# Fused block attention, gated MoE and routed experts on one core: the fourth group's scores from f16 halves, the weight preparation written later, and new anchors for work on ScalarE and VectorE

## The chip, the cores and the metric

The kernel runs on one core of a Trainium2 chip. The metric is the device time of one execution in microseconds (us); lower is better. TensorE (PE) multiplies matrices, VectorE (DVE) and ScalarE (ACT) do elementwise work and reductions, GpSimd (POOL) and SyncE (SP) mostly issue transfers (DMA). Engines run side by side and wait for each other by semaphores.

## What is computed

```python
def reference(**kwargs):                      # q, k, v: (8, 8, 576, 64)
    attn_out = _attn_ref(**attn_kwargs)       # softmax(q k^T / 8 + block mask) v, blocks of 64
    B, H, S, D = attn_out.shape
    x = np.ascontiguousarray(attn_out.transpose(0, 2, 1, 3)).reshape(B * S, H * D)   # 4608 x 512
    x = _moe_ref(x=x, **moe_kwargs)           # ((x @ w1) * (x @ w2)) @ w3 @ w_out
    return _moe2_ref(x=x, **moe2_kwargs)      # logits = x @ w_gate; each token goes to one of 8
                                              # experts by capacity; relu(x @ w1[e]) @ w2[e]
```

Inputs and outputs are f32.

## The kernel before

The first half of the program (to about 722 us) holds the attention and the products with w1 and w2. Attention is cut into 32 head pairs `n` (four for each of the eight batches `b`), and each pair into two parts, which gives 64 half steps `h`. A half step makes scores on TensorE (`tiles`, tile S in PSUM, two buffers), takes the row maxima on VectorE (`maxima`, tile nb), exponentials with row sums on ScalarE (`exp`, tile E), and splits the normalised result into an f16 high half (`high`, mostly ScalarE) and an f16 low half (`low_`, VectorE), both in tile P. A DMA transposes P (`transP`, tile PT), and about a half step later TensorE multiplies PT by v (`pv`, tile PV). That product is split in turn into halves of tile xT: ScalarE writes the high half, then VectorE the low half (`lo`). When all four pairs of a batch are there, `moe_unit` multiplies xT by one 128-column block of w1 and of w2 (24 matmuls, three f16 products per block of the contraction), ScalarE copies one result (`copy_`, tile a_sb) and VectorE multiplies it with the other (`gate_`, tile g). There are 128 such units, two in most half steps. They and the small products of `total` share three PSUM buffers named ab.

q and k come in groups of two pairs (`GROUPS`, `load_qk`, tile qk32, two buffers). Groups below `GF` use the f32 data as they are, in one f32 product. From group `GF` on, `qk_scale` squares q and k on ScalarE (`sq`, tile junk), lets TensorE add up the sums over partitions (`total`, a product with a tile of ones, reading tile qm), makes a power-of-two scale on VectorE (`fin`, tile qp), and splits q and k into f16 halves: `high_half` on ScalarE and `low_half` on VectorE (tile qkT). The scores are then three f16 products. The same squares, totals and splits serve v (`scale_v`, `prep_v`), w_out (`wo_chunk` decodes and squares it, `wo_half` splits it, `wo_turn` turns it by DMA) and w3 (`w3_chunk`); `w34` multiplies the two and writes W3 x w_out to memory for later.

The order of the work is written by hand in units of half steps. `at(p, f)` puts f at place p, `defer(d, f)` at d after the present place, and the program is emitted in order of these places. From half step `HS` = 14 on, TensorE's own order is exactly this one. The other engines' orders come from a scheduler that may move an instruction ahead of others. `behind(key, f)` binds it: what f issues stays behind the newest instruction that is kept under that key ("a" the copy of a unit, "g" its gate, "m" the maxima, "e" the exponentials). `spread` puts ScalarE and VectorE pieces at one of the two places of each half step that `PLACES` lists, each bound behind its key.

The last half of the program (routing of the tokens and the experts) is not touched.

## Time and profile before

| | us |
|---|---|
| median of three runs | 1444.08 (1442.85 to 1445.35) |
| the profiled execution | 1445.89 |
| its span in the trace | 1444.2 |

The span is the time from the first to the last recorded instruction. The profiled execution is a run of its own, 1.8 us above the median. A busy engine is one with an instruction in flight. A row of a wait names the engine that was idle and the instruction of another engine that ended the idle time. The granted clock is 1.00 where TensorE runs at 2.4 GHz throughout and 0.50 where it runs at 1.2 GHz.

### The profile page before, as it was taken

To read this page: it belongs to the slowest core of one execution; us is meant where nothing else is said; L and a number is where in the kernel's file an instruction comes from. 1 tells how busy PE (TensorE), PEld (TensorE's weight loads), DVE (VectorE), ACT (ScalarE), POOL (GpSimd) and SP (SyncE) were. 2 spreads that over 40 slices of the span, in tenths; PEclk is the share of its full clock that TensorE was granted. 3 is DMA by queue.
4 is the path that set the end of the run, shared out by engine and by line. 5 is a ranking of instruction groups with operands and counts; after the bars stand their busy time and mean duration, and the time that the engine had idled before them with its cause. 6 is when DMAs were issued, how large, how long until landed. Compare 5 with 4: busy or idle time off the path is not lost. (4 is left out here: it accounts for less than half of the span.)

```text
span 1444.2 us, 31956 instructions
## 1 busy us (share of the span) xinstructions
PE 1316.7 (91%) x12461; PEld 909.5 (63%) x12461; DVE 963.7 (67%) x2866; ACT 950.7 (66%) x2223; POOL 114.5 (8%) x136
## 2 busy tenths in 40 slices
PE   4689779899999999999999899999889999999997
PEld 3356457676767666766776566666576566666663
DVE  7998788788878888777514577777454456354530
ACT  7887787878878788776634465455346667675641
POOL 0000000000000000010001111111032211110001
PEclk6789999999999999999999999999989999999999
DMA  9888779887978876698999978979585686565200
GB/s 287 199 180 198 182 161 203 180 186 170 175 180 166 190 199 137 149 224 212 227 287 227 234 171 211 203 206 202 154 155 142 158 199 144 177 161 153 74 30 37
DMA packets 383814, 257.45 MB, mean 178 GB/s; under 512 B 260784, under 2 KB 344752, under 8 KB 382640
## 3 DMA queue, kind: packets, MB, share of 16 engines
q1 hardware_dynamic: 370464, 213.44, 62.1%
q0 software_dynamic: 11520, 39.87, 12.3%
q8 instruction: 97, 1.59, 0.5%
q10 hardware_dynamic: 1680, 2.11, 0.4%
q14 instruction: 53, 0.43, 0.1%
HBM read 130.84 MB, written 39.86 MB: 118 GB/s over the span
## 5 line engine op out<-in xcount | busy, mean ns | idle before, releaser
L453 PE MATMUL ab<-xT,w1h 128*128 128x288 f16 x1536 | 218.8, 292 | 20.4 <-DVE xT L429 14.0
L453 PE MATMUL ab<-xT,w2h 128*128 128x288 f16 x1536 | 214.5, 290 | 3.6 <-ACT w34o L718 2.0
L1333 PE MATMUL pe<-xT,ewa 128*128 128x288 f16 (+2 forms) x1728 | 193.0, 275 | 1.6 <-ACT xT L1301 0.9
L453 PEld LDWEIGHTS <-w1h 128*128 128x128 f16 x1536 | 148.3, 101 | 67.8 <-issue 26.6
L1351 PE MATMUL pe<-ewb,h 128*128 128x512 f16 (+1 forms) x960 | 189.3, 379 | 0.0
L453 PEld LDWEIGHTS <-w2h 128*128 128x128 f16 x1536 | 152.4, 99 | 46.2 <-issue 5.2
L1333 PEld LDWEIGHTS <-ewa 128*128 128x128 f16 x1728 | 157.7, 99 | 36.1 <-issue 2.0
L369 DVE SCALAR_TENSOR_TENSOR P<-E,rr,P 128x128 f16<-128x128 f32 (+4 forms) x288 | 155.7, 575 | 15.5 <-ACT P L365 15.4
L1351 PEld LDWEIGHTS <-h 128*128 128x128 f16 (+1 forms) x960 | 85.4, 101 | 98.8 <-issue 2.6
L349 ACT ACTIVATE E<-S,nb,cc 128x384 f32<-128x384 f32 (+4 forms) x216 | 136.3, 639 | 2.1
L365 ACT ACTIVATE P<-E,rr 128x384 f16<-128x384 f32 (+2 forms) x224 | 121.2, 603 | 8.2 <-DVE rr L354 2.1
L1141 PE MATMUL px<-W34h,gh 128*128 128x512 f32 x288 | 120.0, 417 | 3.3 <-ACT gh L1162 3.3
L1141 PE MATMUL px<-W34h,gl 128*128 128x512 f32 x288 | 119.8, 416 | 3.5 <-DMA gl<-g 3.5
L1141 PE MATMUL px<-W34l,gh 128*128 128x512 f32 x288 | 119.5, 415 | 0.0
L341 DVE TENSOR_REDUCE nb<-S 128x2 f32<-128x768 f32 (+3 forms) x128 | 101.1, 814 | 3.8 <-PE S L327 3.4
L423 PE MATMUL PV<-PT,v 128*64 128x128 f16 (+1 forms) x2880 | 88.2, 218 | 16.8 <-DMA PT<-P 15.7
L423 PEld LDWEIGHTS <-v 128*64 128x64 f16 x2880 | 77.3, 114 | 35.2 <-issue 27.2
L1336 DVE SCALAR_TENSOR_TENSOR h<-pe,h 128x288 f16<-128x288 f32 (+2 forms) x144 | 57.7, 419 | 46.9 <-ACT h L1335 46.0
L1354 ACT ACTIVATE y<-pe,s 128x512 f32<-128x512 f32 x36 | 24.7, 687 | 95.0 <-PE pe L1351 65.8
L1291 DVE SCALAR_TENSOR_TENSOR x<-xg,xsc,x 128x512 f16<-128x512 f32 x36 | 27.1, 751 | 84.0 <-ACT x L1290 84.0
L1335 ACT ACTIVATE h<-pe 128x288 f16<-128x288 f32 (+2 forms) x144 | 52.6, 377 | 44.5 <-PE pe L1333 41.6
L1159 ACT ACTIVATE gl<-g 128x1024 fp32r<-128x1024 f32 x36 | 37.9, 1056 | 64.7 <-DMA g<-gd 64.7
(298 smaller groups left out, 2255.6 us busy)
## 6 DMA issues: line engine op xcount, KB each, us to landing
g<-gd SPq DMA_DIRECT2D x36, 512.0 KB, 5.5
gl<-g POOLq DMA_DIRECT2D x36, 512.0 KB, 5.6
raw<-in_moe_w_dram SPq DMA_DIRECT2D x32, 512.0 KB, 4.7
esa<-in_moe_w_dram SPq DMA_DIRECT2D x8, 2048.0 KB, 9.9
esb<-in_moe_w_dram SPq DMA_DIRECT2D x8, 2048.0 KB, 11.3
gd<-g SPq DMA_DIRECT2D x56, 288.0 KB, 3.5
g<-gd SPq DMA_DIRECT2D x14, 1152.0 KB, 7.8
v<-in_v_dram SPq DMA_DIRECT2D x8, 1280.0 KB, 6.7
```

Source lines behind the costliest of these rows:

```text
L341: newest["m"] = nc.vector.tensor_reduce(nb[:, 0, x:x + 2], ps[:, :, o:o + N], axis=AX.X, op=ALU.max)
L349: newest["e"] = nc.scalar.activation(d["e"][:, cols[x]], pf_[:, cols[x]], AF.Exp, bias=nb[:, 1, x:x + 1], scale=c[:, 0:1], accum_out=sums[ ...
L365: nc.scalar.activation(hi, d["e"][:, cols[x]], AF.Copy, scale=r[:, 1, x:x + 1])
L369: nc.vector.scalar_tensor_tensor(lo, d["e"][:, cols[x]], r[:, 1, x:x + 1], hi, op0=ALU.mult, op1=ALU.subtract)
L423: nc.tensor.matmul(ps[hh * 64:hh * 64 + 64, c0:c0 + w], vt[:, zv, hh, j, :], s, start=z == 0 and j == 0, stop=z == 2 and j == nj - 1)
L453: nc.tensor.matmul(p[:, :288], w[:, zw, cc, :], x[:, zx, cc, c0:c0 + 288], start=first, stop=cc == 3 and zw == 1)
L1141: nc.tensor.matmul(p, gh[a][:, f], W34[b][:, f], start=f == 0 and a + b == 0, stop=f == 7 and a == 1)
L1159: nc.scalar.activation(gh[1], g, AF.Copy, scale=-1.0)
L1333: nc.tensor.matmul(p[:, :n], w1[:, a, cc, f * P:(f + 1) * P], t[:, 4 * b + cc, x], start=cc == 0 and a + b == 0, stop=cc == 3 and a == 1)
L1335: nc.scalar.activation(h[:, 0, f, x], p[:, :n], AF.Relu)
L1336: nc.vector.scalar_tensor_tensor(h[:, 1, f, x], p[:, :n], 0.0, h[:, 0, f, x], op0=ALU.max, op1=ALU.subtract)
L1351: nc.tensor.matmul(p[r0:r1], h[:, a, f, k_ * P + r0:k_ * P + r1], EW[e, "b"][0][:, b, f], start=f == 0 and a + b == 0, stop=f == 7 and a == 1)
```

## The change

`GF` goes from 4 to 3, so the fourth group (pairs 6 and 7, half steps 10, 11, 14 and 15) is split into halves and scored by three f16 products; `qk_scale` for it is written at place 8.2. The scale of group 4 moves from 13.95 to 14.42, that of group 5 from 16.4 to 14.95, and those of the later groups by a tenth. Group 4's squares, and the pieces that ScalarE gets by `spread`, are now bound behind the exponentials ("e", place .42) or behind xT's high half ("x", place .07) instead of behind the copies of a unit. The first maxima of a half step are bound behind xT's low half ("xl"). The decode, split and turn of w_out, the decode of w3 and `w34` are written six to seven half steps later, with w3 at 3.2 half steps a chunk instead of 4.

```diff
--- before.py
+++ after.py
@@ -26,7 +26,7 @@
 TS = 13
 HS = 14
 UL = 112
-GF = 4
+GF = 3
 DVE_HI = (2,), (2,)
 TH = 5
 TB = 15
@@ -158,7 +158,7 @@
         with tc.issue_after(newest[key].ins):
             f(*a)
 
-    PLACES = {"a": ((.42, "a"), (.76, "a")), "g": ((.3, "m"), (.58, "g")), "g5": ((.58, "g"), (.92, "g"))}
+    PLACES = {"a": ((.07, "x"), (.42, "e")), "g": ((.3, "m"), (.58, "g")), "g5": ((.58, "g"), (.92, "g"))}
 
     def spread(key, p, f, *a, soon=False):
         p = max(p, now[0])
@@ -187,7 +187,7 @@
             else:
                 spread(key, now[0] + .1, low_half, soon=key != "g")
 
-        spread("a", p, high_half)
+        spread("a", p, high_half, soon=key != "g")
 
     gate = {}
     qk32, qkT, vhl, xT, PT = {}, {}, {}, {}, {}
@@ -277,7 +277,7 @@
                                                op0=ALU.mult, op1=ALU.mult)
             for z in range(2):
                 split(T[:, z, 0, :w], T[:, z, 1, :w], qk32[g][:, z, :w], s[:, z:z + 1], .14,
-                      then=lambda: end(d2), key="g5" if g == 5 else "g")
+                      then=lambda: end(d2), key="g5" if g == 4 else "g")
             pq[g] = s, c, T
 
         done = []
@@ -293,9 +293,9 @@
             if g + 2 < len(GROUPS):
                 load_qk(g + 2)
 
-        if g == 5:
-            defer(.02, behind, "a", sq, 0)
-            defer(d0, behind, "a", sq, 1)
+        if g == 4:
+            defer(0, behind, "e", sq, 0)
+            defer(.02, behind, "e", sq, 1)
             return
         spread("a", now[0], sq, 0)
         spread("a", now[0] + d0, sq, 1)
@@ -369,7 +369,10 @@
                 nc.vector.scalar_tensor_tensor(lo, d["e"][:, cols[x]], r[:, 1, x:x + 1], hi, op0=ALU.mult,
                                                op1=ALU.subtract)
 
-            defer(nb_at, maxima)
+            if now[0] > HS + 1 and nb_at < .15:
+                defer(nb_at, behind, "xl", maxima)
+            else:
+                defer(nb_at, maxima)
             for x in range(k_):
                 defer(ex_at + .05 * x, exp, x)
                 defer(hi_at + .02 * x, high, x)
@@ -426,11 +429,14 @@
         x = xT[b]
 
         def lo():
-            nc.vector.scalar_tensor_tensor(x[:, 1, hp, i0 * 64:i1 * 64], ps[:, :w], 2.0 ** -TS,
-                                           x[:, 0, hp, i0 * 64:i1 * 64], op0=ALU.mult, op1=ALU.subtract)
+            newest["xl"] = nc.vector.scalar_tensor_tensor(x[:, 1, hp, i0 * 64:i1 * 64], ps[:, :w], 2.0 ** -TS,
+                                                          x[:, 0, hp, i0 * 64:i1 * 64], op0=ALU.mult, op1=ALU.subtract)
             held.remove("v")
 
-        defer(.12, lambda: nc.scalar.activation(x[:, 0, hp, i0 * 64:i1 * 64], ps[:, :w], AF.Copy, scale=2.0 ** -TS))
+        def hi():
+            newest["x"] = nc.scalar.activation(x[:, 0, hp, i0 * 64:i1 * 64], ps[:, :w], AF.Copy, scale=2.0 ** -TS)
+
+        defer(.12, hi)
         defer(.13, lo)
 
     lg, lgT, gg = {}, {}, {}
@@ -700,7 +706,7 @@
             m = sm.tile([P, 1], F32, name="w3m")
             wo["T", f] = wo["p3"].tile([P, 2, 1024], F16, name="w3h", bufs=2)
             spread("a", now[0], ssq, w3, m, wo["T", f][:, 1])
-            defer(.8, total, m, .06, use)
+            defer(.7, total, m, .06, use)
 
         decode(("3", f, h), w3[:, h * 512:h * 512 + 512], squares if h else lambda: None)
 
@@ -802,24 +808,25 @@
         at(8 * b + 4.5, scale_x, b)
         at(8 * b - 1.4 if b else .34, scale_v, b)
         if b + 1 < B:
-            at(8 * b + (4.1 if b < 2 else 5.35), load_v, b + 1)
-    for p, g in ((6.1, 2), (8.1, 3), (13.1, 4), (16.1, 5)):
+            at(8 * b + (4.1 if b < 2 else 5.62), load_v, b + 1)
+    for p, g in ((5.1, 2), (7.1, 3), (13.05, 4)):
         at(p, load_qk, g)
-    at(13.95, qk_scale, 4, .1, .5, 0)
-    at(16.4, qk_scale, 5, .36, .3, 0)
+    at(8.2, qk_scale, 3, .15, .3, 0)
+    at(14.42, qk_scale, 4, 0, .56, 0)
+    at(14.95, qk_scale, 5, .3, .6, 0)
     for g in range(6, len(GROUPS)):
         b = g // 2 - 1
-        at(8 * b + (6.9 if g % 2 else 4.9), qk_scale, g, .3, .6 if g % 2 else .45, 1.02)
+        at(8 * b + (7 if g % 2 else 5), qk_scale, g, .3, .62, 0)
     for f in range(8):
         at(2 + .7 * f, prep_w, f)
-        at(9.2 + .75 * f, wo_chunk, f)
-        at(16.2 + .25 * f, wo_half, f)
-        at(18.4 + .5 * f, wo_turn, f)
-        at(23.5 + 4 * f, w3_chunk, f, 0)
-        at(24.9 + 4 * f, w3_chunk, f, 1)
-        at(27.58 + 4 * f, w34, f)
-    at(15.8, wo_split)
-    at(22.95, wo_gate)
+        at(16.2 + .75 * f, wo_chunk, f)
+        at(22.6 + .25 * f, wo_half, f)
+        at(26.2 + .5 * f, wo_turn, f)
+        at(29.6 + 3.2 * f, w3_chunk, f, 0)
+        at(30.6 + 3.2 * f, w3_chunk, f, 1)
+        at(int(33.28 + 3.2 * f) + .42, w34, f)
+    at(22.2, wo_split)
+    at(30.8, wo_gate)
     at(55.97, late_open)
     for h in range(UL // 8):
         at(56.6 + .9 * h, alone, "l", late_run, h)
```

TensorE, around the sum of group 4's squares (`ab<-qm,ones`): w1h_73 is the first weight tile of the second unit in half step 14, w1h_74 that of the first unit in half step 15. Before:

```order
L423 LDWEIGHTS v_1061
L423 MATMUL PV<-PT_2100,v_1061 64x64
L145 MATMUL ab<-qm,ones 128x2
L453 LDWEIGHTS w1h_73
L453 MATMUL ab<-xT,w1h_73 128x288
```

and after the change:

```order
L387 LDWEIGHTS q_108
L387 MATMUL S<-qkT,q_108 128x64
L145 MATMUL ab<-qm,ones 128x2
L459 LDWEIGHTS w1h_74
L459 MATMUL ab<-xT,w1h_74 128x288
```

The sum stood ahead of the second unit of half step 14; now it stands behind that unit and behind the scores of half step 15.

ScalarE in half step 14, from its exponentials on (`E` 128x576). Tile qk_2128 is group 4's, wo is w_out, dec a decoded weight. Before:

```order
L349 ACTIVATE E,sums<-S,nb,c_110 128x576
L197 ACTIVATE wo_1480,wom<-wo_1478 128x512
L365 ACTIVATE P_120<-E,rr 128x576
L563 ACTIVATE dec<-raw 128x512
L365 ACTIVATE P_120<-E,rr 128x512 x2
L197 ACTIVATE junk,qm<-qk_2128 128x1152
L365 ACTIVATE P_119<-E,rr 128x576
L433 ACTIVATE xT<-PV 128x192
L197 ACTIVATE junk,qm<-qk_2128 128x1152
L463 ACTIVATE a_sb<-ab 128x288
L197 ACTIVATE v_2305,vm<-v_121 128x1024
L184 ACTIVATE qkT<-qk_2128,qp 128x1152 x2
```

After the change, where group 4's tile is qk_2107:

```order
L349 ACTIVATE E,sums<-S,nb,cc 128x576
L197 ACTIVATE junk,qm<-qk_2107 128x1152
L469 ACTIVATE a_sb<-ab 128x288
L197 ACTIVATE wo_2528,wom<-wo_2526 128x512
L365 ACTIVATE P_120<-E,rr 128x512 x2
L569 ACTIVATE dec<-raw 128x512
L365 ACTIVATE P_119<-E,rr 128x576
L197 ACTIVATE junk,qm<-qk_2107 128x1152
L469 ACTIVATE a_sb<-ab 128x288
L437 ACTIVATE xT<-PV 128x192
L197 ACTIVATE v_2274,vm<-v_121 128x1024
L347 ACTIVATE nb<-nb,cc 128x2
```

The first square stands directly behind the exponentials and the second behind as many instructions as before. Nine instructions further down the order goes on, with the last of the exponentials of half step 15, the third square of v, group 5's first square (`qk_1458`) and only then group 4's two upper halves (`qkT<-qk_2107`):

```order
L349 ACTIVATE E,sums<-S,nb,cc 128x576
L197 ACTIVATE v_2274,vm<-v_121 128x1024
L197 ACTIVATE junk,qm<-qk_1458 128x1152
L184 ACTIVATE qkT<-qk_2107,qp 128x1152 x2
L469 ACTIVATE a_sb<-ab 128x288
```

Between the second square and these two halves there is now the work of a whole half step; before, there were two instructions.

VectorE at the start of half step 38, where batch 4's first unit waits for xT (the same at 30, 46 and 54). `nb<-S` are maxima, `xT<-PV,xT` is the low half. Before:

```order
L696 TENSOR_TENSOR w3f<-w3p,wgee 128x1
L341 TENSOR_REDUCE nb<-S 128x2
L369 SCALAR_TENSOR_TENSOR P_120<-E,rr,P_120 128x576
L343 TENSOR_REDUCE nb<-S 128x1
L429 SCALAR_TENSOR_TENSOR xT<-PV,xT 128x384
L77 TENSOR_SCALAR qp<-ab 128x2
```

and after the change:

```order
L702 TENSOR_TENSOR w3f<-w3p,wgee 128x1
L432 SCALAR_TENSOR_TENSOR xT<-PV,xT 128x384
L341 TENSOR_REDUCE nb<-S 128x2
L77 TENSOR_SCALAR qp<-ab 128x2
L343 TENSOR_REDUCE nb<-S 128x1
L179 SCALAR_TENSOR_TENSOR w3h<-w3d,w3p,w3h 128x1024
```

xT's low half has moved ahead of both maxima.

## Rows read from the trace of the kernel before

**Rows 1.** The page's first line.

```profile
span 1444.2 us, 31956 instructions
```

**Rows 2.** Stretches: length, busy us of each engine (x its instructions), granted clock, DMA.

```profile
core 0: us, PE busy (x) PEld busy (x) DVE busy (x) ACT busy (x) POOL busy (x), PEclk, DMA share, GB/s
0.00:158.97 158.97, 114.74 (x1112) 78.24 (x1113) 142.20 (x356) 128.37 (x331) 1.60 (x11) 0.83 0.87 214
158.97:228.22 69.25, 52.59 (x619) 38.19 (x620) 52.77 (x130) 53.91 (x129) 0.00 (x0) 0.90 0.78 173
228.22:291.60 63.38, 57.37 (x734) 43.88 (x731) 48.88 (x134) 50.86 (x121) 0.00 (x0) 0.95 0.95 193
291.60:365.62 74.02, 70.94 (x834) 51.02 (x832) 63.55 (x160) 61.17 (x148) 0.00 (x0) 1.00 0.80 180
365.62:623.88 258.26, 244.61 (x2964) 177.17 (x2959) 213.25 (x541) 213.10 (x519) 1.77 (x10) 1.00 0.76 167
623.88:721.85 97.97, 92.43 (x1144) 65.68 (x1138) 67.21 (x169) 62.84 (x167) 4.35 (x3) 0.97 0.98 231
...
170.80:176.40 5.60, 5.49 (x28) 3.65 (x28) 0.63 (x5) 2.02 (x5) 0.00 (x0) 0.60 0.48 89
...
201.90:206.80 4.90, 4.86 (x27) 3.28 (x28) 3.67 (x18) 4.83 (x17) 0.00 (x0) 0.65 0.55 139
...
216.20:220.80 4.60, 4.60 (x28) 3.04 (x25) 3.22 (x7) 1.98 (x7) 0.00 (x0) 0.63 1.07 268
```

**Rows 3.** Waits of PE, 158.9 to 721.9 us: total us, times, longest.

```profile
PE ab L453 <- DVE xT L429: 14.0, 9, 4.7
PE ab L145 <- ACT junk L197: 9.6, 2, 5.0
```

**Rows 4.** Waits of ACT, the same stretch and columns.

```profile
ACT nb L347 <- DVE nb L341: 71.0, 49, 6.3
```

**Rows 5.** Timeline of PE, half steps 14 to 18: start us, us, what, [idle before].

```profile
170.91 0.59 PE L145 MATMUL ab<-qm,ones 128*128 128x2 f32 x2 [5.02 <-ACT junk L197]
...
178.53 1.63 PE L453 MATMUL ab<-xT,w1h 128*128 128x288 f16 x12
...
201.94 0.38 PE L145 MATMUL ab<-qm,ones 128*128 128x2 f32 x2 [4.60 <-ACT junk L197]
...
215.53 0.50 PE L323 MATMUL S<-qkT 64*128 64x384 f16 x4 [2.79 <-DVE qkT L179]
```

**Rows 6.** Timeline of ACT, half steps 14 to 17.

```profile
163.72 0.83 ACT L349 ACTIVATE E<-S,nb,c 128x576 f32<-128x576 f32 x1
...
169.60 1.16 ACT L197 ACTIVATE junk<-qk 128x1152 f16<-128x1152 f32 x1
...
175.78 2.39 ACT L184 ACTIVATE qkT<-qk,qp 128x1152 f16<-128x1152 f32 x2
...
191.62 0.72 ACT L184 ACTIVATE wo<-wo,wop 128x512 f16<-128x512 f32 x1
...
196.77 1.16 ACT L197 ACTIVATE junk<-qk 128x1152 f16<-128x1152 f32 x1 [1.03 <-DMA qk<-in_q_dram]
```

**Rows 7.** Groups by shape on PE, 80 to 240 us: count, busy us, mean ns.

```profile
L323 PE MATMUL S<-qk 64*128 64x384 f32 x16 | 4.0, 576 | 0.9 <-ACT E L349 0.9
L323 PE MATMUL S<-qkT 64*128 64x384 f16 x24 | 2.8, 323 | 3.6 <-DVE qkT L179 2.8 <-ACT qkT L184 0.8
```

**Rows 8.** Timeline of PE: w34 in half step 35, units in 38 and 58.

```profile
397.95 5.34 PE L713 MATMUL ab<-wo,w3h 128*128 128x512 f16 x24
...
430.92 0.41 PE L453 MATMUL ab<-xT,w1h 128*128 128x288 f16 x2 [1.64 <-DVE xT L429]
...
651.61 0.64 PE L453 MATMUL ab<-xT,w1h 128*128 128x288 f16 x2 [4.67 <-DVE xT L429]
```

**Rows 9.** Timeline of ACT at the start of half step 38.

```profile
428.16 0.48 ACT L433 ACTIVATE xT<-PV 128x384 f16<-128x384 f32 x1
```

**Rows 10.** Timeline of DVE, the same place.

```profile
427.80 1.22 DVE L341 TENSOR_REDUCE nb<-S 128x2 f32<-128x1024 f32 x1
...
430.32 0.55 DVE L429 SCALAR_TENSOR_TENSOR xT<-PV,xT 128x384 f16<-128x384 f32 x1
```

## The prediction

> **What bounds the kernel now.** I read the table of stretches first [rows 2]. Until 159 us VectorE is busy for 142.2 us of 159.0, and TensorE for 114.7; the order of TensorE is not yet the written one there. From 158.97 (the scores of half step 14) to 721.85 us TensorE is the bound: it is idle for 69.25 − 52.59 = 16.7, 63.38 − 57.37 = 6.0, 3.1, 13.7 and 5.5 us in the five stretches A to E, 45.0 us together, while VectorE and ScalarE are busy for three quarters to seven eighths of each. The granted clock adds a loss: (1 − 0.90) × 69.25 = 6.9 us in A, 3.2 in B (0.95), 2.9 in E (0.97), none in C and D. This is an upper bound, since some of it falls on idle time. So 45.0 + 13.0 = 58 us is all that better order can give back there, and what comes after 721.85 us (722.4 of the span's 1444.2 [rows 1, 2]) is not touched.
>
> Then I asked who ended TensorE's waits [rows 3]. The largest is VectorE's low half of xT: 14.0 us in nine waits. Next are the squares of groups 4 and 5: 9.6 us in two waits, 5.02 and 4.60 [rows 5]. What follows these two and the wait of 2.79 us for group 5's halves [rows 5] is dear too: TensorE ran at 0.60 for 5.60 us, at 0.65 for 4.90 and at 0.63 for 4.60 [rows 2], that is 2.2, 1.7 and 1.7 us lost behind them.
>
> **The change, part by part.**
>
> *Until 159 us.* Group 3's split adds two squares and two upper halves to ScalarE, 2 × 1.16 + 2.39 = 4.7 us by the rows of group 4 [rows 6], and two lower halves to VectorE; these have no row here, and by the upper ones they are about 2.4. The work on w_out is written seven half steps later, but VectorE and ScalarE have no written order: by the order lists all but one or two of its eight chunks still stand ahead of half step 14, so little leaves this stretch. The scores get cheaper: 16 f32 records of one size cost 4.0 us and the 24 f16 ones of as many products 2.8 [rows 7], each from four pairs, so 0.3 us a pair at 768 of its 3136 columns, 1.2 us for a pair and 2.4 for the two, half of it here. I take 0 for the stretch: −3 if VectorE is relieved of the chunks that left, +4 if ScalarE's 4.7 us end last.
>
> (The Trainium skill, "Perfetto Trace Analysis", section "Engine Utilization", halves TensorE's peak for FP32_LOW_HIGH. If that is what f32 costs, one f32 product is worth two f16 ones and three halves' products cost half as much again: 768 columns would go from 1.0 to 1.5 us, two pairs would cost 4.1 us more instead of 2.4 less, and the sum would end 6.5 us higher. The rows read the other way, 1.0 against 0.7, so I go by them.)
>
> *Stretch A, half steps 14 to 18.* Group 4's sum moves from ahead of the second unit to behind that unit and the scores of half step 15. ScalarE's second square ended at 169.60 + 1.16 = 170.76, 6.2 us behind the exponentials' end (163.72 + 0.83 = 164.55) [rows 6]; by the new order it ends about as late. TensorE meanwhile has a unit (two times 1.47 us, from records of 12 that overlap a little [rows 5]), a product with v and scores to do, some 6 to 7 us. So the 5.02 us and the 2.2 behind it go. Group 5's data is loaded as soon as group 3's halves are made, so ScalarE's wait for the transfer of 1.03 us [rows 6] goes and both squares stand earlier; with them the 4.60 and 1.7 us, and the 2.79 and 1.7 for its halves. The turn of w_out leaves this stretch, and its waits with it.
>
> Something is late next: group 4's upper halves now stand behind a half step of other ScalarE work, 18 instructions and eight reads of accumulators from the second square to their end. At A's 53.91/129 = 0.42 us each [rows 2] that is 10.9 us, so 17 us behind the exponentials, and 18.3 with the last lower half. TensorE is at the scores that need them after 7 + two units + a product with v and the other scores, about 15. I put 3.5 us of wait there, 1.9 us of lower clock behind it (as behind the others), and 2 us for the next two half steps, in which group 5's halves crowd the same engines. Idle time and clock were 16.7 + 6.9 = 23.6. The three waits are 12.4 of it and the clock behind them 5.6; of the other 5.6 I let half stay, 2.8. So 23.6 − 7.4 − 2.8 = 13.4 come back, and 1.2 from the scores. I take −13; the ends are −20 (the halves are in time) and −5 (the new wait is as long as the old ones).
>
> *Stretch B, to half step 25.* Here 6.0 + 3.2 = 9.2 us could come back. But the splitting of w_out moves in: eight upper halves of 0.72 us on ScalarE [rows 6], 5.8 us, where it had 63.38 − 50.86 = 12.5 idle. Half comes back: −4.5, between −9 and +2.
>
> *Stretch C.* 3.1 us idle, half of it back: −1.5. Two `w34` of 5.34 us [rows 8] leave C and come back in D, and the small products of the turn enter C from B: nothing in the sum.
>
> *Stretch D, half steps 32 to 56.* In half step 38 TensorE waited 1.64 us for xT's low half [rows 8]. ScalarE's half was done at 428.16 + 0.48 = 428.64 [rows 9], but VectorE began at 427.80 with maxima, and came to the low half at 430.32 [rows 10]. The new order puts it ahead of both maxima: it could begin at 428.64 and end at 429.2, where TensorE comes to need it at 429.3 (430.92 − 1.64). So the nine waits [rows 3] go but for the last, of 4.67 us. About 14.0 − 4.67 = 9.3 us, 7.4 of it in D, the rest in C. What the waiting maxima cost: ScalarE waits for maxima already, 71.0 us in 49 times [rows 4], 1.4 us a time. That is a bubble that the pieces bound behind xT's high half now fill, and TensorE, with two score buffers, has most of a half step in hand. I take −7 of 13.7 us; ends −11 and +3.
>
> *Stretch E.* The wait of 4.67 us [rows 8] stands behind constants of the routing that the scheduler put on VectorE; they now stand half a step earlier. 5.5 + 2.9 = 8.4 us are there; I take −4, between −8 and 0.
>
> Sum: 0 − 13 − 4.5 − 1.5 − 7 − 4 = −30. The profiled execution took 1445.89, so 1415.9; it was 1.8 above the median, so 1414 beside the median of 1444.08.
>
> **The rivals.**
>
> *Nearly all of it goes.* If ScalarE and VectorE keep up everywhere, as their 75 to 88% leave room for, three quarters of 58 us come back: 1444.1 − 43.5 = 1401. Against it: group 4's halves by the count above.
>
> *ScalarE is the next bound.* In A and B it is busy for 104.8 of 132.6 us [rows 2] and gets the splits of w_out on top; if each wait that goes comes back as a wait for a late piece of ScalarE's, A and B give 5 together, C and D 4, E 3: 1432. The mixed places "x" and "e" speak for it, the idle 71 us ahead of the maxima against it.
>
> *The binding of the maxima costs more than all else gives (slower).* Every half step from 16 on has its first maxima behind xT's low half, that behind xT's high half, and that behind the product with v. If ScalarE and VectorE are late by a half step, the chain of high half, low half, maxima, exponentials holds the score buffers, and each of 49 half steps pays 0.48 + 0.55 us [rows 9, 10]: +50 − 30, 1464. It decides from 30/49 = 0.6 us a half step that reaches TensorE. (The Trainium skill, "TensorE: Matmul & The Clock Gate", section "Architectural detail", has ScalarE and VectorE as strict FIFO, so all behind a bound instruction waits with it; the waits in rows 4 are such.) Against it: TensorE's lead, and that maxima are no later than now wherever xT is split in time.
>
> *Nothing moves.* The scheduler had already put most of this work into gaps; if the waits only change their names, the time stays within 0.2%, which is about what a measurement of this kernel can tell: 1441 to 1447.
>
> **How the numbers follow.** Forecast 0.52, nearly all 0.18, ScalarE 0.17, maxima 0.08, nothing 0.05. The first three are faster by over 0.2%: 0.87; same 0.05; slower 0.08. The forecast's own ends, A's and D's above all, reach from 1402 to 1426; with ScalarE's case and half of the first rival inside, the range is 1399 to 1436, which leaves out the maxima, nothing and some 0.07 of the first.
>
> **What would show it.** Right: no wait of TensorE for junk over 2 us in half steps 14 to 18, a wait for qkT of 2 to 5 us at half step 16, under 3 us of waits for xT from half step 19 to 56, the scores of half step 14 at 156 to 163 us and those of half step 19 about 13 us earlier relative to them. Wrong: the waits for nb or E on TensorE grow to tens of us (the maxima), or ab waits for a_sb in most half steps of B (ScalarE), or half step 14 comes later than 163 us, which would mean that the first stretch pays for group 3's split.

## The result and the profile after

The changed kernel takes 1465.62 us (median of four runs, 1463.3 to 1467.39). In the same session the kernel before took 1444.43. The ratio is 1.0147, 95% interval 1.0129 to 1.0165: 21 us slower, where 30 us faster was forecast. The profiled execution took 1463.3 us with this span, which answers to [rows 1]:

```profile
span 1461.6 us, 31982 instructions
```

The stretches of the changed kernel are cut at the same instructions as in [rows 2] (columns as there). The two stretches behind 721.85 us of the kernel before, which were not shown ahead of the prediction, stand under them.

```profile
0.00:158.32 158.32, 111.85 (x1126) 77.16 (x1126) 141.55 (x358) 129.75 (x329) 1.61 (x11) 0.88 0.84 216
158.32:213.68 55.36, 47.61 (x617) 35.34 (x615) 46.68 (x114) 49.58 (x125) 0.00 (x0) 0.97 0.89 199
213.68:276.43 62.75, 55.26 (x678) 41.20 (x675) 50.18 (x123) 52.60 (x123) 0.00 (x0) 0.97 0.64 141
276.43:355.27 78.84, 65.61 (x818) 48.67 (x817) 60.70 (x165) 59.25 (x150) 0.00 (x0) 0.96 0.96 193
355.27:631.73 276.46, 260.30 (x3046) 185.73 (x3041) 223.22 (x566) 221.30 (x529) 1.65 (x10) 0.98 0.68 163
631.73:727.37 95.64, 91.44 (x1145) 65.57 (x1139) 67.18 (x169) 63.10 (x167) 4.33 (x3) 0.98 1.01 242
727.37:1061.24 333.87, 305.59 (x2354) 210.56 (x2353) 200.51 (x887) 155.60 (x280) 34.78 (x40) 0.97 0.81 204
1061.24:1461.60 400.36, 380.89 (x2722) 245.67 (x2722) 175.57 (x497) 225.28 (x529) 72.08 (x72) 0.97 0.50 130
```

```profile
721.85:1042.86 321.01, 302.61 (x2354) 209.11 (x2353) 200.25 (x887) 155.52 (x280) 34.88 (x40) 0.99 0.87 212
1042.86:1444.20 401.34, 381.43 (x2722) 246.22 (x2722) 175.57 (x497) 224.89 (x529) 71.91 (x72) 0.98 0.51 129
```

Stretch by stretch, after less before: −0.7, A −13.9, B −0.6, C and D together +23.0 (355.30 against 332.28; they are taken together because two `w34` went from the one to the other), E −2.3, the stretch behind it +12.9, the last −1.0; sum +17.4. So A did what was forecast, and the loss has two places: C with D, and a stretch that the prediction had called not touched.

In C and D TensorE is idle for 78.84 − 65.61 + 276.46 − 260.30 = 29.4 us, against 16.7 in [rows 2], and its clock is 0.96 and 0.98 where it was 1.00. So 12.7 of the 23.0 us are idle time; in the other 10.4 TensorE is busy for longer, of which the lower clock explains at most 0.04 × 78.84 + 0.02 × 276.46 = 8.7 us (an estimate). The waits of TensorE in the changed kernel from 158.3 to 727.4 us, to be read against [rows 3]:

```profile
PE ab L145 <- ACT w3h L197: 9.2, 3, 5.1
PE ab L459 <- ACT a_sb L469: 7.0, 3, 4.0
PE ab L459 <- DVE xT L432: 4.5, 4, 1.5
PE ab L145 <- ACT junk L197: 4.4, 4, 2.6
PE ab L513 <- DMA g<-gd: 3.5, 1, 3.5
PE ab L145 <- ACT w34o L724: 3.2, 2, 2.4
PE ab L145 <- ACT v L197: 3.1, 2, 1.8
...
PE S L323 <- DVE qkT L179: 1.3, 1, 1.3
...
PE S L323 <- ACT qkT L184: 1.0, 1, 1.0
```

The waits for xT fell from 14.0 to 4.5 us and those for junk from 9.6 to 4.4, as the prediction said. In their place stand waits for ScalarE: the squares of w3 (w3h), the copies a_sb, and w34's copy (w34o). This is one of them, half step 31, ScalarE and then TensorE:

```profile
346.72 1.04 ACT L197 ACTIVATE v<-v 128x1024 f16<-128x1024 f32 x1
...
347.76 1.04 ACT L197 ACTIVATE w3h<-w3d 128x1024 f16<-128x1024 f32 x1
...
348.80 1.15 ACT L197 ACTIVATE junk<-qk 128x1152 f16<-128x1152 f32 x1
...
350.19 2.00 ACT L365 ACTIVATE P<-E,rr 128x512 f16<-128x512 f32 x3
```

```profile
348.95 0.47 PE L145 MATMUL ab<-w3m,ones 128*128 128x1 f32 x2 [5.13 <-ACT w3h L197]
```

The three squares stand between the exponentials and P, where the new places put them. TensorE's hand-written order has the total of w3 there, .7 of a half step behind the decode, and comes to it 5.13 us too early.

Behind 727 us one row of waits is new, 15.5 us in two waits:

```profile
PE ab L459 <- ACT a_sb L469: 15.5, 2, 10.8
```

ScalarE's timeline there shows why. Changed kernel:

```profile
746.83 1.04 ACT L1135 ACTIVATE W34h<-w 128x1024 fp32r<-128x1024 f32 x1
747.78 0.39 ACT L469 ACTIVATE a_sb<-ab 128x288 f32<-128x288 f32 x1
748.07 0.39 ACT L521 ACTIVATE lgT<-ab 128x288 f32<-128x288 f32 x1
760.71 1.06 ACT L1166 ACTIVATE gl<-g 128x1024 fp32r<-128x1024 f32 x1 [12.25 <-DMA g<-gd]
...
763.57 1.04 ACT L1169 ACTIVATE gh<-g 128x1024 fp32r<-128x1024 f32 x1
764.52 0.39 ACT L469 ACTIVATE a_sb<-ab 128x288 f32<-128x288 f32 x1
```

Kernel before, the same place of the program:

```profile
748.19 1.05 ACT L1124 ACTIVATE W34l<-w 128x1024 fp32r<-128x1024 f32 x1
749.13 1.05 ACT L1128 ACTIVATE W34h<-w 128x1024 fp32r<-128x1024 f32 x1
750.82 0.41 ACT L463 ACTIVATE a_sb<-ab 128x288 f32<-128x288 f32 x1 [0.64 <-PE ab L453]
751.13 1.05 ACT L1124 ACTIVATE W34l<-w 128x1024 fp32r<-128x1024 f32 x1
752.07 1.05 ACT L1128 ACTIVATE W34h<-w 128x1024 fp32r<-128x1024 f32 x1
```

Before, a piece of W34 or two follow each a_sb, because `load_w34` and `prep_g` call `spread("a", ...)` too and "a" bound their pieces behind the newest a_sb. The change binds them behind the newest xT and the newest exponentials. The last of these come with the end of the attention (the last xT of ScalarE at 739.35 us), so from there on nothing holds the pieces back: all eight of W34 and four of g stand ahead of an a_sb, and the first piece of g waits 12.25 us for its transfer with that a_sb behind it. (The Trainium skill, "TensorE: Matmul & The Clock Gate", section "Architectural detail", has ScalarE as strict FIFO; this wait is what the rule says.)

### The profile page after: what moved, and what is told of

It is laid out like the page before. It is cut to its first block, busy times and chain, and to the rows that moved or that the text cites. A ratio compares the mean times of both kernels' runs of the same rounds, so it can differ in the third digit from the quotient of the medians.

```text
span 1461.6 us, 31982 instructions
## 1 busy us (share of the span) xinstructions
PE 1318.6 (90%) x12483; PEld 909.9 (62%) x12483; DVE 965.6 (66%) x2873; ACT 956.5 (65%) x2229; POOL 114.4 (8%) x136
## 5 line engine op out<-in xcount | busy, mean ns | idle before, releaser
L349 ACT ACTIVATE E<-S,nb,cc 128x384 f32<-128x384 f32 (+4 forms) x234 | 148.1, 640 | 2.2
L426 PE MATMUL PV<-PT,v 128*64 128x128 f16 (+1 forms) x2880 | 89.4, 219 | 15.5 <-DMA PT<-P 13.3
L1183 ACT ACTIVATE jk<-px 128x512 f16<-128x512 f32 x36 | 21.4, 595 | 92.7 <-issue 64.2
```

The source lines that it names most:

```text
L349: newest["e"] = nc.scalar.activation(d["e"][:, cols[x]], pf_[:, cols[x]], AF.Exp, bias=nb[:, 1, x:x + 1], scale=c[:, 0:1], accum_out=sums[ ...
L426: nc.tensor.matmul(ps[hh * 64:hh * 64 + 64, c0:c0 + w], vt[:, zv, hh, j, :], s, start=z == 0 and j == 0, stop=z == 2 and j == nj - 1)
```

## The experiments

Each run was timed in three rounds (e16 in five) beside the kernel before on the same chip; the ratio is to that kernel, with its 95% interval. Medians of different sessions differ by a microsecond or two, so the ratios are what is compared: 0.001 is 1.4 us. To place a difference, I read from each trace when VectorE starts the first maxima of half steps 14, 25, 57 and 63 and when TensorE starts the first product of the experts. The lengths between, in us:

```
run                            to h14  h14-24  h25-56  h57-62  h63 to    experts   ratio to before
                                                               experts
before                         161.7   129.9   345.9    68.6   348.1     390.1     1
changed                        159.5   119.8   370.7    61.6   360.5     389.6     1.0147
e1_pieces_undone               160.4   119.8   355.3    68.1   345.8     389.5     0.9985
e2_tail_pieces                 160.8   119.5   370.8    62.1   346.4     390.7     1.0031
e3_weights_undone              158.7   125.2   353.8    61.6   359.2     390.8     1.0043
e4_maxima_undone               158.7   117.6   370.3    61.2   357.7     390.5     1.0109
e5_no_pieces_no_weights        161.3   127.2   345.8    68.3   346.6     390.9     0.9969
e6_w3_totals_later             158.1   119.8   364.3    62.0   349.5     389.8     0.9978
e7_weights_undone_tail         160.2   123.4   351.4    62.2   345.8     390.2     0.9933
e8_scores_alone                161.2   126.6   350.5    69.5   348.4     390.5     0.9998
e9_decode_bound                159.5   118.9   363.9    61.3   346.8     390.0     0.9997
e10_weights_alone              162.3   124.7   359.7    67.8   345.4     389.6     1.0072
e11_turns_later                159.5   123.6   354.8    61.3   345.7     390.4     0.9953
e12_scores_undone              161.0   124.6   366.6    61.7   362.9     390.7     1.0176
e13_w34_next_step              161.3   122.9   362.5    61.3   345.9     390.5     1.0012
e14_maxima_undone_tail         158.9   126.7   349.3    61.9   346.3     389.5     0.9920
e15_weights_between            159.6   125.3   359.7    61.3   344.8     390.8     1.0001
e16_places_by_step             162.4   125.4   345.2    60.8   345.9     390.3     0.9898
e17_places_new_weights         159.6   120.5   363.3    60.8   347.5     390.1     0.9993
e18_places_no_maxima           160.1   125.6   350.8    60.7   346.3     389.7     0.9951
```

Each row comes from one execution, the profiled one, which can lie some us off the median. How far a stage repeats is seen in two pairs: the changed kernel and e2, and e3 and e7, have the same instructions in the same order on TensorE, VectorE and ScalarE up to the first piece of W34 (740 and 727 us); the first two agree to 0.5 us from h14 to h62, but e3 and e7 differ by 1.8 us in h14-24 and 2.4 in h25-56. Differences of this size are not read as effects below. And the cut is at an instruction that the binding of the maxima itself moves: where that binding differs, the whole time says more than a stage.

The theories (their letters are not those of the stretches): A, the new places of ScalarE's pieces cost the time, behind 722 us and in h26 to h55; B, the new times of w3 cost the attention part; C, the maxima's wait does.

**Pieces undone (e1).** All else as changed.

```diff
-    PLACES = {"a": ((.07, "x"), (.42, "e")), ...
+    PLACES = {"a": ((.42, "a"), (.76, "a")), ...
```

> The changed kernel with one part undone: ScalarE's pieces stand behind a_sb copies at .42 and .76 of a half step again, not behind xT's high half and the exponentials. Theory A (the new places cost the time: after 722 us they free the W34 and g pieces from the a_sb copies, which costs about 12 us, and in h26 to h55 they put squares between the exponentials and P, in front of a_sb and w34o, which costs about 15 us): 1435 to 1442 us, no PE wait of over 2 us for a_sb after 722 us and none for w3h at h31 and h47. Theory B (the 3.2 step cadence of w3 with its total at .7 costs the attention part): the tail's 12 us come back, the w3h waits of 5.1 and 3.7 us stay: 1451 to 1455 us. Theory C (maxima behind xT's low half): as B, about 1453 us.

Measured 1442.46 us, ratio 0.9985 (0.9966 to 1.0004). Theory A's time came to half a us, but not all of its signs: the two waits behind 722 us are gone (345.8 us in that stage against 360.5) and 15.4 us of h25 to h56, yet TensorE still waits 3.7 us for w3h at h31 and 3.0 at h47.

**Only the tail's pieces behind a_sb (e2).**

```diff
-    PLACES = {"a": ((.07, "x"), (.42, "e")), ...
+    PLACES = {"a": ((.07, "x"), (.42, "e")), "t": ((.42, "a"), (.76, "a")), ...
-        spread("a", now[0] + 1.0, low_half)          # load_w34; the high half and prep_g alike
+        spread("t", now[0] + 1.0, low_half)
```

> The changed kernel with only the pieces of W34 and of g (all after 722 us) behind the a_sb copies as before; every piece of the attention part as in the changed kernel. If the two a_sb waits of 4.8 and 10.8 us after 722 us come from the places alone: 1465.6 - 12.4 = about 1453 us (1451 to 1456), and the half steps up to h63 as in the changed kernel. If instead the order there is set by when the last w34 is done, the time stays at 1464 to 1467 us.

Measured 1449.75 us, ratio 1.0031 (1.0016 to 1.0046). h14 to h62 is as in the changed kernel to 0.6 us a stage, and the stage from h63 on loses its 14.1 us. So the tail's loss comes from the table of places, and nothing of it is left once these pieces are back (346.4 us, 348.1 before).

**Weights undone (e3).** w_out and w3 at the times of before.

```diff
-        at(29.6 + 3.2 * f, w3_chunk, f, 0)           # and the other lines of w_out, w3 and w34
+        at(23.5 + 4 * f, w3_chunk, f, 0)
```

> The changed kernel with w_out and w3 prepared at the times of before (cadence 4 half steps, total at .8), all else as changed. Theory A: the tail's 12 us and most of the loss of h26 to h55 stay, 1457 to 1466 us. Theory B: the loss of h25 to h56 (about 15 to 20 us against before) goes and the tail's 12 us stay, 1445 to 1452 us.

Measured 1451.25 us, ratio 1.0043 (1.0025 to 1.0061): theory B's. The tail's loss stays, h25 to h56 gives 16.9 us back, and h14 to h24 takes 5.4.

**Maxima undone (e4).** `maxima` without `behind "xl"`.

```diff
-            if now[0] > HS + 1 and nb_at < .15:
-                defer(nb_at, behind, "xl", maxima)
-            else:
-                defer(nb_at, maxima)
+            defer(nb_at, maxima)
```

> The changed kernel without the wait of the maxima for xT's low half. Theory C (this wait delays the exponentials in 49 half steps): 10 us or more faster than the changed kernel, 1448 to 1456 us. Theories A and B: within 4 us of the changed kernel, 1462 to 1470 us, with more PE waits for xT and fewer us for E.

Measured 1460.7 us, ratio 1.0109 (1.008 to 1.0139). The time lies between the two expectations. h25 to h56, where theory C has its price, is the same (370.3 against 370.7); 2.2 us are in h14 to h24 and 2.8 in the tail. Theory C is out as the cause of the loss there.

**Neither pieces nor weights (e5).** The kernel before with the parts on the scores, on the later scales and loads, and on the maxima.

```diff
-GF = 4
+GF = 3                                           # with its loads, scales and keys, and the later
+            ...                                  # qk_scale of groups 6 and up and load_v
+                defer(nb_at, behind, "xl", maxima)
```

> The kernel before with the fourth group's scores from halves, the later scales of groups 6 and up, the later loads of v and the maxima behind xT's low half: without the new weight times and without the new places of ScalarE's pieces. If these two took what the rest gives (theory B for h25 to h56, theory A for the tail): the 11 to 13 us of h14 to h18 are kept to the end and the PE waits for xT of h19 to h56 (14 us in before) shrink, 1428 to 1436 us. If the maxima or the scales of groups 6 and up lose time by themselves: 1440 us or more.

Measured 1441.41 us, ratio 0.9969 (0.9951 to 0.9986). Here I was wrong: of the 11 to 13 us only 2.7 are left at h25. w_out's splitting is back in h16 to h18 on ScalarE, and TensorE waits 4.1 us for an a_sb at h16 (all waits for a_sb from 158 to 735 us):

```profile
PE ab L456 <- ACT a_sb L466: 8.6, 6, 4.1
```

**Totals of w3 later (e6).** On e2_tail_pieces.

```diff
-            defer(.7, total, m, .06, use)
+            defer(1.0, total, m, .06, use)
```

> The changed kernel with the tail's pieces behind a_sb (run e2_tail_pieces, 1449.8 us) and the totals of the w3 squares at 1.0 half steps behind the decode in place of .7. If the two waits for w3h (5.1 us at h31 and 3.7 us at h47) with the lower clock behind them are what the new w3 times cost: both go, 1437 to 1443 us. Rival: the split of w3 comes later by as much and w34 waits for it, 1447 to 1455 us.

Measured 1443.09 us, ratio 0.9978 (0.9957 to 0.9998). The waits at h31 and h47 shrink from 5.1 and 3.7 to 1.6 and 0.8 us, and h25 to h56 gives back 6.5 us. The rest of its loss stays.

**Weights undone, tail's pieces behind a_sb (e7).** The two edits of e2_tail_pieces and e3_weights_undone together.

```diff
-        spread("a", now[0] + 1.0, low_half)
+        spread("t", now[0] + 1.0, low_half)
...
-        at(29.6 + 3.2 * f, w3_chunk, f, 0)
+        at(23.5 + 4 * f, w3_chunk, f, 0)
```

> Run e3_weights_undone (1451.3 us) with the tail's pieces of W34 and g behind a_sb again: 1451.3 - 12.5 = about 1438.5 us (1436 to 1442). Against run e5_no_pieces_no_weights it differs by the new places of ScalarE's pieces in the attention part alone: theory A says 4 us or more slower than that run (w34o waits of 2.4 us at h31, h39 and h47), theory B within 3 us of it.

Measured 1434.91 us, ratio 0.9933 (0.9911 to 0.9954): 10 us faster than before. h25 to h56 is 5.6 us longer than in e5, the run with the old places, as theory A says (8.0 in e3, the same program up to there), but h14 to h24 and h57 to h62 are 3.8 and 6.1 shorter. In h31, h39 and h47 it has this (ScalarE, then TensorE, h31):

```profile
350.22 1.04 ACT L197 ACTIVATE v<-v 128x1024 f16<-128x1024 f32 x1
...
351.26 1.15 ACT L197 ACTIVATE junk<-qk 128x1152 f16<-128x1152 f32 x1
...
352.41 0.66 ACT L569 ACTIVATE dec<-raw 128x512 f32<-128x512 f32 x1
352.98 1.99 ACT L365 ACTIVATE P<-E,rr 128x512 f16<-128x512 f32 x3
354.87 0.66 ACT L724 ACTIVATE w34o<-ab,w3f 128x512 f32<-128x512 f32 x1
```

```profile
355.58 0.39 PE L145 MATMUL ab<-vm,ones 128*128 128x3 f32 x2 [2.37 <-ACT w34o L724]
```

The total of v needs the PSUM bank that w34's copy gives back, and the copy stands behind squares, a decode and P.

**Scores alone (e8).** The kernel before with `GF` = 3, its loads and scales, the later scales of groups 6 and up, and the later loads of v.

```diff
-GF = 4
+GF = 3
...
-        at(8 * b + (6.9 if g % 2 else 4.9), qk_scale, g, .3, .6 if g % 2 else .45, 1.02)
+        at(8 * b + (7 if g % 2 else 5), qk_scale, g, .3, .62, 0)
```

> The kernel before with the scores of the fourth group from halves, the later scales of groups 6 and up and the later loads of v alone. h14 to h18 as in the changed kernel: 10 to 13 us shorter, kept to the end: 1431 to 1437 us; against run e5_no_pieces_no_weights the PE waits for xT in h26 to h54 (1.6 and .8 us in most groups of eight half steps) stay, so that this run is 3 to 8 us slower than that one if the binding of the maxima does what its place says, and no slower if it does nothing.

Measured 1445.88 us, ratio 0.9998 (0.9976 to 1.0019): nothing gained, and 4.5 us more than e5, which is what was said for the maxima's wait (the two intervals overlap a little). 3.3 us come in h14 to h24 and go again in h25 to h56. Of the 10.1 us of h14 to h24 the scores alone bring a third, although the waits for junk and for qkT are gone there: with w_out's work still in place, others stand instead, the longest this one at h16.

```profile
PE ab L453 <- ACT a_sb L463: 5.7, 3, 4.5
```

**Decode bound behind a_sb (e9).** On e6_w3_totals_later.

```diff
-        nc.scalar.activation(a, hi.bitcast(F32), AF.Abs)
+        with tc.issue_after(newest["a"].ins) if key[0] == "3" else ExitStack():
+            nc.scalar.activation(a, hi.bitcast(F32), AF.Abs)
```

> Run e6_w3_totals_later (1443.1 us) with each decode of a w3 chunk placed on ScalarE behind the a_sb copy that precedes it in the program. In that run a_sb copies wait behind a decode that itself waits 5.8 us for its raw transfer, and TensorE waits 2.3 and 2.9 us for a_sb at h26 and h27 at a lower clock behind. If that is the loss of the new weight times in h25 to h28: 5 to 8 us less, 1435 to 1439 us. If the a_sb copies there are late for another reason (DMA of the transposed P, 1.6 us in that place): within 2 us of 1443.

Measured 1443.72 us, ratio 0.9997 (0.9984 to 1.0011): nothing. The two waits for a_sb at h26 and h27 (2.3 and 2.9 us) are gone, but at h31 and h32, where e6 waits 3.1 us, there are now 8.3:

```profile
PE ab L459 <- ACT a_sb L469: 4.0, 1, 4.0
PE ab L145 <- ACT w3h L197: 2.6, 1, 2.6
PE ab L459 <- DVE qp L77: 1.7, 1, 1.7
```

**Weights alone (e10).** The kernel before with the new lines of w_out, w3, w34 and the total at .7.

```diff
-        at(23.5 + 4 * f, w3_chunk, f, 0)
+        at(29.6 + 3.2 * f, w3_chunk, f, 0)
...
-            defer(.8, total, m, .06, use)
+            defer(.7, total, m, .06, use)
```

> The kernel before with the new times of w_out and w3 alone (cadence 3.2, total at .7, w34 at .42). If the new weight times lose by themselves what separates run e7_weights_undone_tail from run e2_tail_pieces (14.8 us): 1455 to 1462 us. If they lose only together with the new places of ScalarE's pieces (runs e1_pieces_undone and e5_no_pieces_no_weights are 1 to 2 us apart): 1442 to 1449 us.

Measured 1452.16 us, ratio 1.0072 (1.0045 to 1.0099), between the two. This program does not compute the reference's values, and which step of the preparation it spoils was not traced. The engines run as many instructions as before (12461, 2866 and 2223 on PE, DVE and ACT), so its time is taken as that of the same work, and nothing below rests on it alone. h14 to h24 is 5.2 us shorter and h25 to h56 13.8 longer than before, without any new place.

**Turns of w_out later (e11).** On e7_weights_undone_tail.

```diff
-        at(18.4 + .5 * f, wo_turn, f)
+        at(19.4 + .5 * f, wo_turn, f)
-    at(22.95, wo_gate)
+    at(24.2, wo_gate)
```

> Run e7_weights_undone_tail (1434.9 us) with the turns of w_out one half step later (19.4 in place of 18.4) and its gate at 24.2. There TensorE waits 3.3 us at h19 for a transposed w_out with a clock of .88 behind it: if the transfer is just late, both go, 1429 to 1432 us. If the wait only moves to the next turn or the queue of SP sets it: 1433 to 1437 us.

Measured 1437.22 us, ratio 0.9953 (0.9935 to 0.9971), as the second expectation says, to 0.2 us. The wait for the turned w_out is gone and h14 to h24 is no shorter (123.6 against 123.4).

**Scores undone (e12).** The changed kernel with `GF` = 4 and its loads and scales.

```diff
-GF = 3
+GF = 4
...
-    at(14.42, qk_scale, 4, 0, .56, 0)
+    at(13.95, qk_scale, 4, .1, .5, 0)
```

> The changed kernel with the fourth group's scores from 32 bit products and its loads and scales as before; all else changed. If h14 to h18 gained their 10.7 us from the scores: 10 to 15 us slower than the changed kernel, 1475 to 1480 us. If the places of the pieces gained it (run e8_scores_alone gains nothing over before): within 4 us of the changed kernel, 1462 to 1469 us.

Measured 1468.68 us, ratio 1.0176 (1.0157 to 1.0194), 3 to 4 us slower than the changed kernel, inside the second expectation. h14 to h24 is 4.8 us longer, with the waits for the squares of groups 4 and 5 back (6.05 and 5.79 us of this row):

```profile
PE ab L145 <- ACT junk L197: 16.1, 6, 6.1
```

**w34 elsewhere (e13).** On e7_weights_undone_tail.

```diff
-        at(27.58 + 4 * f, w34, f)
+        at(min(28.42 + 4 * f, 55.42), w34, f)
```

> Run e7_weights_undone_tail (1434.9 us) with each w34 moved from 27.58 + 4 f to 28.42 + 4 f (the last at 55.42). There TensorE waits 2.4 us at h31, h39 and h47 for the copy of w34's result, because a total that needs the same bank follows it at once while ScalarE still has squares, a decode and P ahead of the copy. If the place of w34 beside that total is the cause: these waits go with the lower clock behind two of them, 1426 to 1431 us. If any place beside ScalarE's pieces has such a wait: 1433 to 1439 us.

Measured 1447.03 us, ratio 1.0012 (0.9996 to 1.0029): 11 us slower, outside of both. Of the waits for w34's copy one of 0.8 us is left, but with w34 gone from in front of it TensorE comes to the total of v some 5 us earlier, and there the squares of v are not done. These are four waits of 4.5 us and less for them:

```profile
PE ab L145 <- ACT v L197: 14.1, 4, 4.5
```

**Maxima undone (e14).** On e7_weights_undone_tail.

```diff
-                defer(nb_at, behind, "xl", maxima)
+                defer(nb_at, maxima)
```

> Run e7_weights_undone_tail (1434.9 us) without the maxima's wait for xT's low half. The two pairs of runs so far differ in sign (without it, the changed kernel is 5 us faster, and run e8_scores_alone, which has neither it nor the sooner pieces, is 4 us slower than run e5_no_pieces_no_weights). If the wait saves TensorE's waits for xT at no cost: 3 to 8 us slower, 1438 to 1443 us. If it costs as in the changed kernel: 1428 to 1432 us. If it is worth nothing that can be measured: 1433 to 1437 us.

Measured 1433.42 us, ratio 0.992 (0.9889 to 0.9952): no difference that can be measured.

**Weights between (e15).** On e6_w3_totals_later.

```diff
-        at(29.6 + 3.2 * f, w3_chunk, f, 0)
-        at(30.6 + 3.2 * f, w3_chunk, f, 1)
-        at(int(33.28 + 3.2 * f) + .42, w34, f)
+        at(26.1 + 3.6 * f, w3_chunk, f, 0)           # w_out 3 to 4 half steps earlier as well
+        at(27.3 + 3.6 * f, w3_chunk, f, 1)
+        at(int(30.2 + 3.6 * f) + .42, w34, f)
```

> Run e6_w3_totals_later (1443.1 us) with w_out 3.5 half steps earlier and w3 at a cadence of 3.6 half steps between those of before and of the change: w3 from h26 in place of h29.6, w34 from h30 in place of h33, the last in h55 in all. If the shorter cadence is what loses the rest (more ScalarE work and more w34 in each half step of h33 to h56): about half of the 8 us between that run and e7_weights_undone_tail comes back, 1437 to 1441 us. If the loss hangs on where single pieces fall in a half step and not on the cadence: outside of that, up to 1450 us.

Measured 1445.62 us, ratio 1.0001 (0.9982 to 1.0019): not the first expectation, but inside the second. h25 to h56 is 4.6 us shorter than in e6, of the 12.9 between e6 and e7, and h14 to h24 gives 5.5 back.

**New places outside of h28 to h53 only (e16, e17, e18).** On e7_weights_undone_tail, then on e6_w3_totals_later, then on e14_maxima_undone_tail.

```diff
-        places = [(x + y, k) for x in range(int(p), int(p) + 3) for y, k in PLACES[key]]
+        places = [(x + y, k) for x in range(int(p), int(p) + 3)
+                  for y, k in PLACES["t" if key == "a" and 28 <= p < 54 else key]]
```

> Run e7_weights_undone_tail (1434.9 us) with ScalarE's pieces of h28 to h53 at the places of before (behind a_sb, .42 and .76) and all others at the new ones. In h33 to h56 run e5_no_pieces_no_weights, with the places of before, took 7.2 us less than that run, which waits 2.4 us at h31, h39 and h47 with a lower clock behind; before h28 and at h57 the new places gained. If the new places lose by these half steps and gain by the others: no such waits, 1425 to 1430 us. If what is saved there comes back as waits for xT or E: 1433 to 1437 us.

Measured 1430.97 us, ratio 0.9898 (0.988 to 0.9915): 14 us faster than before and between the two expectations. It is the best median of all, though the intervals of e7 and e14 overlap its own a little. h25 to h56 is 6.2 us shorter than in e7_weights_undone_tail and the waits at h31, h39 and h47 are gone; the 2 us more in h14 to h24 and 2.2 ahead of h14 are of the size by which equal programs differ. The waits for xT, [rows 3] in the kernel before, are here

```profile
PE ab L459 <- DVE xT L432: 4.0, 5, 1.5
```

> Run e6_w3_totals_later (1443.1 us: the new weight times, tail's pieces behind a_sb, totals at 1.0) with ScalarE's pieces of h28 to h53 at the places of before. If the loss of the new weight times is in fact the new places together with them: the waits for w34o (h39) and a_sb (h40, h48) go, 1434 to 1439 us. If the new weight times lose wherever the pieces stand: 1441 to 1447 us.

Measured 1444.47 us, ratio 0.9993 (0.9978 to 1.0009). h25 to h56 is 363.3 us, hardly less than with the new places (364.3): the new weight times lose wherever the pieces of h28 to h53 stand. How much they lose hangs on more than these: e1, with every piece at its old place, has 355.3 us there.

> Run e16_places_by_step without the maxima's wait for xT's low half: within 3 us of that run, as run e14_maxima_undone_tail was of e7_weights_undone_tail.

Measured 1437.88 us, ratio 0.9951 (0.9931 to 0.997), some 7 us slower than the run with the wait: not as expected. The two profiled executions are only 3.0 us apart, 5.6 more in h25 to h56 and 2.3 less ahead of h14. The waits for xT are back:

```profile
PE ab L456 <- DVE xT L429: 11.8, 8, 1.9
```

## Why the prediction was wrong, step by step

*Until 159 us*: forecast 0, measured −0.7. This tests little: runs of this kind reach h14 anywhere from 158.1 to 162.4 us (table).

*Stretch A*: −13 forecast, −13.9 measured. Part of the mechanism is there: no wait for junk is left in A (the one of 2.6 us stands in B), and TensorE waits 2.3 us for group 4's halves (the two rows on qkT above) where 3.5 were put. These halves came 18.3 and 20.0 us behind the exponentials where 17 and 18.3 were said, but TensorE was there only after 17.4, not 15. Where the gain comes from was misjudged, and that the number fits is in part luck: I gave nearly all of it to the three waits. In e8, which has this part alone, they go and h14 to h24 gains 3.3 us; with the maxima's binding it is 2.7 (e5), and with the new times of the weights on top, the pieces still at their old places, 10.1 (e1), as much as in the changed kernel. The weights alone gain 5.2 with two waits for junk still there (e10, 5.0 and 4.0 us). So the departure of w_out's work, priced at 2.8 us, is over half of the gain, and the new places of the pieces are not needed for it.

*Stretch B*: −4.5 forecast, −0.6 measured, inside its ends. TensorE's idle time grew from 6.0 to 7.5 us, with new waits for junk (3.3 us) and E (2.1).

*Stretches C and D*: −8.5 forecast, +23.0 measured. This is the first step that failed. The wait for xT was judged rightly: most of it goes. What its going is worth depends on the rest. Four pairs of runs differ in nothing but the binding of the maxima: with the pieces of h28 to h53 at their old places it brings 4.5 and 6.9 us of the whole time (e8 to e5, e18 to e16), with all pieces at the new places nothing (e14 to e7, 1.5 us the other way) or a loss (e4 to the changed kernel, 4.9). No single stage shows this safely: cut at TensorE's first product of 384 columns in h25 and in h56, the same pairs differ by 1.5 and 4.1 us of gain, 3.4 of loss and 0.2 of gain. What failed are two sentences that costed moved work at nothing: that the 71 us of ScalarE's idle time ahead of the maxima are "a bubble that the pieces bound behind xT's high half now fill", and that the two `w34` and the products of the turn that move within or into C and D are "nothing in the sum". C and D took in 6.3 us more of ScalarE's busy time and 7.1 of VectorE's (the ACT and DVE columns of the stretches) and grew by 23.0. With the pieces and the weights each at their old and new place, h25 to h56 is 345.8 us (both old, e5), 351.4 (new places, e7), 355.3 (new weight times, e1) and 370.8 (both, e2): +5.6, +9.5, and another 9.9 for the two together (with e3 for e7: +8.0, +9.5 and 7.5). An engine with idle time is not enough. TensorE's order is written by hand, each total is a product that waits for a square on ScalarE, and each unit waits for an a_sb; a piece that is put in front of these delays TensorE wherever TensorE gets there first, as at h31 above, however idle ScalarE is later.

Of the 19.4 us that the new weight times cost beside the new places, the totals at .7 are 6.5 (e6). The rest is not settled. Waits that I took away came back as others within a few half steps (e9), and the run between the two cadences lies between in h25 to h56 (e15), which fits a loss by closer work but moves other things too. e1 and e17 have the new weight times and the old places in h28 to h53 and still differ by 8.0 us there; they differ in the totals (.7 and 1.0), in the places of all other pieces and in when an upper half is written, and no run separates these.

*Stretch E*: −4 forecast, −2.3 measured, inside its ends; no wait for xT of over 1.5 us is left. (The prediction's "three quarters to seven eighths" of VectorE's and ScalarE's busy time does not hold for E, where [rows 2] give 69 and 64%.)

*Behind 721.85 us*: 0 forecast (what comes there "is not touched"), +11.9 measured. This is the second step that failed, and it was a reading error: I followed the table of places through `split` and the squares and not through its other two callers. e2 and e7 each show 13 to 14 us for it.

Of the signs that I had named, all those for "right" are there (half step 14 at 158.32 us, half step 19 13.9 us earlier relative to it, the waits for junk, qkT and xT), and none of those for "wrong". The list looked only where gains were expected; it had none for the half steps that receive the moved work.

Against the rivals: the maxima's case had 1464 us, close to what came, by another mechanism; so that is luck: undoing the binding takes back 4.9 us of 21 (e4), and e18 shows it as a gain. ScalarE as the next bound was the right kind, but it took 12.5 us from the gain of A and B and 4.5 from that of C and D, and still forecast a faster kernel.

## What to carry to other kernels

Before a table that many callers read is changed, list all callers and ask each what its entry waits for at the end of the loop: an anchor that has no newer instance holds nothing back. A piece that moves on an engine in program order is priced by what stands behind it there and by which product of TensorE's written order needs that next, not by the engine's idle time. A product that looks like a cost may be the cover of a later wait: moving w34 away took the time that the squares of v needed (e13).

## What the hardware showed that was not expected

The clock behind a stall. These are stretches of 5 us right behind the three equal waits of e7_weights_undone_tail (2.37, 2.37 and 2.36 us, at h31, h39 and h47, the same work behind each; columns as in [rows 2]):

```profile
355.60:360.60 5.00, 5.00 (x96) 3.98 (x97) 4.83 (x13) 2.88 (x8) 0.00 (x0) 1.00 1.19 165
442.60:447.60 5.00, 5.00 (x84) 3.50 (x85) 4.03 (x11) 1.91 (x5) 0.00 (x0) 0.66 1.16 170
530.40:535.40 5.00, 4.90 (x83) 3.44 (x84) 4.29 (x11) 2.41 (x7) 0.00 (x0) 0.68 1.11 204
```

The granted clock stayed at 1.00 (2.4 GHz) once and fell twice, at a loss of 1.7 and 1.6 us (0.34 and 0.32 × 5). In the changed kernel it was 0.66 for 5 us behind the wait of 5.13 us (1.7 us), 0.55 for 5.6 behind one of 3.74 at h47 (2.5 us), and 0.72 for 7 behind that of 10.76 (2.0 us):

```profile
349.00:354.00 5.00, 5.00 (x28) 3.57 (x28) 3.03 (x9) 3.60 (x7) 0.00 (x0) 0.66 0.57 156
...
535.20:540.80 5.60, 5.60 (x26) 3.79 (x27) 2.74 (x8) 3.37 (x6) 0.00 (x0) 0.55 0.47 74
...
765.00:772.00 7.00, 7.00 (x48) 4.21 (x48) 1.08 (x3) 0.82 (x2) 0.00 (x0) 0.72 1.00 226
```

So a wait of 2.4 us can cost as much on top as one of 5 us, or nothing, and the longest of these did not cost the most. What decided it in the three equal cases no run here shows.
